# Spectral mixing and a low-rank MLP on one core: x of batches 2 and 3 issued behind a copy of batch 1's a tiles, steps at later slots, x in eight-row pieces

## The chip, the core and the metric

The kernel runs on one core of a Trainium2 chip. A core has a matrix engine (TensorE, PE in the profile, with its weight loads as PEld), a vector engine (VectorE, DVE), an activation engine (ScalarE, ACT), a general engine (GpSimd, POOL) and SyncE (SP), which issues transfers. Each engine works through its own instructions in their order and waits on semaphores for the others. Transfers are issued by SP, ACT or POOL; those issued by POOL form one queue, and POOL alone can change the type of the data on the way. The metric is the device time of one execution in microseconds.

## The reference

For eight batches of x with 3136 rows of 256 values, in float32:

```
X = rfft(x, axis=1);  Y = X * (filt_r + 1j*filt_i);  y = irfft(Y, n=3136, axis=1)
h = (y^T @ U @ V)^T            # U: 3136 x 32, V: 32 x 3136, along the rows
u = y + h
out = u + relu(u @ w_ch1) @ w_ch2      # 256 -> 1024 -> 256
```

## The kernel before

**The transform.** A row number is 49 q + r, with 64 values of q and 49 of r. The transform over q is a product with a constant 64x64 matrix, the one over r a product with one matrix for each of 32 frequencies s. The inverse goes the other way. Everything inside is float16.

**The path of a batch (1 to 7).** It has these stages, and a tile between each two:

- *load_x(b, c)* (lines 147 to 163): a batch's x comes in three chunks c of 8, 8 and 9 positions (`CH`). A tile `xt` has q on 64 partitions for one half h of the positions and 64 for the other. POOL issues one transfer for each half, since the type changes. Position k of half h holds row r = 8*(k//4) + 4*h + k%4 of each q, so that one half's chunk of eight is two pieces of four rows. There are five `xt` buffers.
- *f1_units(b)* (lines 451 to 471): thirteen units, four for each of the first two chunks and five for the last. A unit is one matmul on two positions (`pf`, line 460), and ACT or DVE copies it to `asb`. Behind the last unit of a chunk `asb` is written to the DRAM tensor c1 (line 470), by SP for batch 1 and by POOL for the others.
- *load_a(b, gi)* (lines 477 to 481): SP reads c1 back, the other way round, as four tiles `a` of eight frequencies each. Each has 768 pieces of 512 bytes and a small second transfer; there are three buffers.
- *stream()* (lines 526 to 557): sixteen *pairs* for each batch, one for two frequencies. A pair is the forward product over r (`px`, line 499, one bank of PSUM), the product with the filter on DVE (line 507 for batch 1, lines 518 to 524 for the others, there with a sum on POOL), and, `LAG` = 2 pairs later, the inverse over r (`pi`, line 535), which ACT copies to `esb`. After every fourth pair `esb` is written to the DRAM tensor c2. `stream` is one generator over all batches: each call of `next` makes a pair and the inverse of two pairs before, so the last two inverses of a batch come with the first two pairs of the next.
- *load_e(b, gi)* (lines 483 to 492): SP reads c2 back as the two tiles `e2`.
- *h1_unit(b)* (lines 563 to 600): the product with U, on all of `e2`.
- *make_u* and the MLP: a batch's rows come in six groups of 512 columns. make_u finishes the inverse over q and adds the low-rank part in the same matmul (line 620; lines 629 and 635 for batch 0). mm1 (line 694) makes eight blocks of h, which ACT or DVE passes through relu, and mm2 (line 720, or 765 from batch 2 on) makes the output, which DVE evicts and POOL or SP stores.

**Batch 0** goes another way at the start (`first_f1`, `first_mid`), while the tables, the filters and the weights are loaded. There x of batch 1 is loaded too, V is loaded into two further `xt` buffers (`vq`), and `v_order` (lines 277 to 288) rearranges V with fourteen copies on POOL into `low`. Chunk 0 of batch 2 is issued in the midst of these copies. Copies of w2 follow (line 812).

**The order of the work** is written out by hand. The last loop goes through the groups: for each of four values of a, it emits two blocks of mm1, runs one *slot*, emits mm2 of the group before, and runs a second slot. So a group is eight slots and a batch is `SB` = 48. `put(slot, gen)` hangs one step of a generator on a slot, rounded to the nearest; the steps of one slot run in the order in which they were put. `steps` holds the slots of the pairs; the units, the loads and the h1 steps are put relative to it or at slots of their own:

```
steps = [8.8 + 1.25 * k for k in range(NP)] + [28 + 2.45 * k for k in range(NP)]
...
put(4 + 1.1 * k if b == 2 else 18 + 2.8 * k if b == 3 else t0 - 54 + 3 * k, fill)
...
put(6 * c - 5 if b == 2 else 9 + 8 * c if b == 3 else t0 - 72 + 12 * c, one(load_x, b, c))
```

Slot 0 runs behind the first mm1 of batch 0's first group, at about 55 us of the profile. What a step emits goes to the end of each engine's queue. Seven copies on POOL (line 560) fill the rest of `low`, at slots 8 to 26.

Of the kernel before, what the change touches and what calls it, by code (L numbers as in the profile page):

```python
# [9 lines left out]
F16 = mybir.dt.float16  # L10
# [3 lines left out]
SEQ = 3136  # L14
NQ, NR = 64, 49
NS = 32
# [3 lines left out]
NH = 25  # L20
# [6 lines left out]
def _consts():  # L27
    n, half = SEQ, SEQ // 2
    r = np.array([8 * (k // 4) + 4 * h + k % 4 for h in range(2) for k in range(NH - h)])
    q = np.arange(NQ)  # L30


    w = np.zeros((NQ, NS, 2))
    for s in range(NS):
        w[:, s, 0] = np.cos(2 * np.pi * s * q / NQ)
        w[:, s, 1] = -np.sin(2 * np.pi * s * q / NQ)
    w[:, 0, 1] = (-1.0) ** q
    w = w.reshape(NQ, 64)
    turn = np.arange(64).reshape(4, 16).T.ravel()
    w64 = np.zeros((128, 128))  # L40
    w64[:64, :64] = w
    w64[64:, 64:] = w
    s2 = np.zeros((128, 128))
    s2[:64, :64] = w.T / ESC
    s2[64:, 64:] = w.T / ESC


    t2 = np.zeros((NS, 98, 128))
    g = np.zeros((NS, 128, 98))
    for s in range(NS):  # L50
        for j in range(49):
            if j < 25:
                f = s + 64 * j
                e, sg = np.exp(-2j * np.pi * f * r / n), 1.0
            elif s:
                f = 64 * (j - 24) - s
                e, sg = np.exp(-2j * np.pi * (n - f) * r / n), -1.0
            else:
                f = 32 + 64 * (j - 25)
                e, sg = np.exp(-2j * np.pi * f * r / n), 1.0  # L60
            ei = np.conj(e)
# [12 lines left out]
    t2[0, :, 64] = 0  # L74
    t2[0, 49:, 64] = (-1.0) ** r
# [14 lines left out]
def kernel(  # L90
# [56 lines left out]
    def load_x(b, c, parts=None):  # L147
        if c not in st[b].setdefault("x", {}):
            st[b]["x"][c] = sb.tile([128, 9 * DM], F16, tag="xt", bufs=5, name="xt")
        t = st[b]["x"][c]  # L150
        for lo, hi in parts or ((c0[c], c0[c + 1]),):
            for h in range(2):
                m = (hi - lo) // 4
                nc.gpsimd.dma_start(  # L154
                    t[64 * h:64 * h + 64, (lo - c0[c]) * DM:(lo - c0[c] + 4 * m) * DM]
                    .rearrange("p (m e) -> p m e", m=m),
                    bass.AP(tensor=x.tensor, offset=x.offset + (b * SEQ + 2 * lo + 4 * h) * DM,
                            ap=[[RD, NQ], [8 * DM, m], [1, 4 * DM]]))
# [113 lines left out]
    wp = cst.tile([128, 128], F16)  # L272
    nc.sync.dma_start(wp, wp_d.ap())
    ul = cst.tile([64, NR * RANK], F16)
    hz = [cst.tile([96, DM], F16, tag=f"hz{k}", name="hz") for k in range(2)]

    def v_order():
# [199 lines left out]
    def load_a(b, gi):  # L477
# [2 lines left out]
            nc.sync.dma_start(t[p:p + n].rearrange("p (k d) -> p k d", d=DM), spec(c1[b], gi, p, n))  # L480
        st[b].setdefault("a", {})[gi] = t

    def load_e(b, gi, ks=(0, 1)):
        for k in ks:
            e2 = new_e2(b, k)
            rows_ = c2[b].ap()[16 * gi:16 * gi + 16]
            nc.sync.dma_start(
                e2[gi:64:4, 0:24 * DM].rearrange("p (h e) -> p h e", h=2),
                bass.AP(tensor=c2[b], offset=16 * gi * RD + 12 * k * DM,
                        ap=[[RD, 16], [NH * DM, 2], [1, 12 * DM]]))  # L490
            if k:
                nc.sync.dma_start(e2[gi:64:4, 24 * DM:NH * DM], rows_[:, 24 * DM:NH * DM])
# [33 lines left out]
    def stream():  # L526
        pend = []

        def i1(b, m, y, esb):
            pi = bank("f", "pi")  # L530
            nf = 2 if b == 1 else 1
            for sl in range(2):
                for fi in range(nf):
                    g, o = (fi * NS + 2 * m + sl) * 98, fi * 512 + sl * DM
                    nc.tensor.matmul(pi[0:98, sl * DM:(sl + 1) * DM], g12[:, g:g + 98],  # L535
                                     y[:, o:o + DM], start=(fi == 0), stop=(fi == nf - 1),
                                     skip_group_check=True)
            gi, ml = divmod(m, KG // 2)
            nc.scalar.copy(split(esb[:, ml * 512:(ml + 1) * 512]), natural(pi[0:98, :]))  # L539
            if ml == KG // 2 - 1:  # L540
                for p, n in ((0, 96), (96, 2)):
                    (nc.scalar if b == 1 else nc.sync).dma_start(
                        spec(c2[b], gi, p, n), esb[p:p + n].rearrange("p (k d) -> p k d", d=DM))

        for b in range(1, nb):
            for m in range(NS // 2):
                gi, ml = divmod(m, KG // 2)
                if ml == 0:
                    esb = sb.tile([98, KG * DM], F16, tag="esb", bufs=2, name="esb")
                y = (both_products if b == 1 else product)(m, forward(m, st[b]["a"][gi], ("x",)))  # L550
                if len(pend) == LAG:
                    i1(*pend.pop(0))
                pend.append((b, m, y, esb))
                yield
        for p in pend:
            i1(*p)
            yield

    def one(load, *a):
        load(*a)  # L560
        yield
# [227 lines left out]
    def put(slot, gen):  # L789
        sched.setdefault(int(slot + 0.5), []).append(gen)  # L790
# [13 lines left out]
    nc.vector.tensor_copy(ft[64:65, 0:DM], nyq[64:65, :])  # L804
    for m in range(3):
        first_a(m)
    vgen = v_order()
    for k, _ in enumerate(vgen):
        if k == 3:
            load_x(2, 0)  # L810
    for h in range(2):
        nc.gpsimd.tensor_copy(split(w2)[:, :, h], natural(w2n)[:, :, h])
    fill = f1_units(1, True)
# [8 lines left out]
    for k in range(2):  # L822
        put(k, fill)

    steps = [8.8 + 1.25 * k for k in range(NP)] + [28 + 2.45 * k for k in range(NP)]
    for b in range(3, nb):
        steps += [SB * (b - 2) + 18 + 3 * k for k in range(NP)]
    steps += [steps[-1] + 3 * (k + 1) for k in range(LAG)]
    mid = stream()
    for b in range(1, nb):  # L830
        gen = h1_unit(b)
        for t in (8, 7, 6) if b > 1 else (9, 8, 7):
            put(SB * b - t, gen)
    for k, t in enumerate(steps):
        put(t, mid)
        b, m = divmod(k - LAG, NP)
        if k >= LAG and m % GP == GP - 1:
            t += 6 if b > 1 or not b and m < NP - 1 else 4
            late = SB * b + 13
            if b and t < late:  # L840
                put(max(t, SB * b - 1), one(load_e, b + 1, m // GP, (0,)))
                put(late, one(load_e, b + 1, m // GP, (1,)))
            else:
                put(t, one(load_e, b + 1, m // GP))
    for b in range(1, nb):
        for gi in range(NS // KG):
            t = steps[NP * (b - 1) + GP * gi]
            put(max(2, t - (14 if b > 3 else 9 + b // 3)), one(load_a, b, gi))
        if b > 1:
            fill = f1_units(b, b == 2)  # L850
            t0 = steps[NP * (b - 1)]
            for k in range(NF):
                put(4 + 1.1 * k if b == 2 else 18 + 2.8 * k if b == 3 else t0 - 54 + 3 * k, fill)
            for c in range(len(CH)):
                if b > 2 or c > 0:
                    put(6 * c - 5 if b == 2 else 9 + 8 * c if b == 3 else t0 - 72 + 12 * c, one(load_x, b, c))

    for k in range(7):
        put(8 + 3 * k, one(
# [55 lines left out]
```

## Time and profile before

| | |
|---|---|
| median of 3 runs | 535.67 us (532.67 to 537.13) |
| the profiled execution | 534.16 us, its span 532.4 us |
| busy: PE, DVE, ACT, POOL | 498.4, 400.7, 377.7, 290.9 us |
| the chain that ended last | PE 79%, DVE 6%, POOL 6%, DMA 6% |
| wait of PE's `pf` for xt | 3.0 us in 2 times, the longest 1.9 |
| moved by POOL's queue, by SP's | 41.91 MB, 49.75 MB |
| HBM read and written | 56.25 and 48.17 MB, 196 GB/s over the span |

In a timeline, each row has the start, the time taken, the engine, the line, the operation and tiles, and the number of instructions merged into it; in brackets stands how long the engine had been idle before it, and what ended that. L460 is line 460 of the kernel before. "SPq" is SP as an issuer of transfers. A row of a stretch has its length, and for PE, PEld, DVE, ACT and POOL the busy time with the number of instructions, then the granted clock of PE (1.00 is full), the busy share of the DMA engines and GB/s.

### The profile page before, as it was taken

To read this page: it belongs to the slowest core of one execution; us is meant where nothing else is said; L and a number is where in the kernel's file an instruction comes from. 1 tells how busy PE (TensorE), PEld (TensorE's weight loads), DVE (VectorE), ACT (ScalarE), POOL (GpSimd) and SP (SyncE) were. 2 spreads that over 40 slices of the span, in tenths; PEclk is the share of its full clock that TensorE was granted. 3 is DMA by queue.
4 is the path that set the end of the run, shared out by engine and by line. 5 is a ranking of instruction groups with operands and counts; after the bars stand their busy time and mean duration, and the time that the engine had idled before them with its cause. 6 is when DMAs were issued, how large, how long until landed. Compare 5 with 4: busy or idle time off the path is not lost.

```text
span 532.4 us, 11368 instructions
## 1 busy us (share of the span) xinstructions
PE 498.4 (94%) x4022; PEld 303.0 (57%) x4022; DVE 400.7 (75%) x574; ACT 377.7 (71%) x771; POOL 290.9 (55%) x412
## 2 busy tenths in 40 slices
PE   3877799999999999999999999989999999999995
PEld 3765266667667785555555555545555555454444
DVE  7897367757786758898998888978999877445663
ACT  2767756677678868888788878877777678765541
POOL 7797633345656456586677665765756564313000
PEclk9979989999999999999999999999999999999999
DMA  8989998986988577897989798896887575544324
GB/s 127 193 150 188 204 211 210 217 223 147 232 234 214 141 154 221 208 229 171 225 204 220 195 240 205 177 235 145 199 194 148 126 180 128 140 96 80 78 66 104
DMA packets 118426, 93.98 MB, mean 177 GB/s; under 512 B 52977, under 2 KB 100786, under 8 KB 118370
## 3 DMA queue, kind: packets, MB, share of 16 engines
q0 software_dynamic: 21936, 41.91, 38.3%
q1 hardware_dynamic: 93226, 49.75, 37.7%
q10 hardware_dynamic: 3208, 1.61, 1.1%
q8 instruction: 31, 0.51, 0.4%
q14 instruction: 25, 0.20, 0.1%
HBM read 56.25 MB, written 48.17 MB: 196 GB/s over the span
## 4 chain that ended last, share of the span: by engine, by line
PE 79%; DVE 6%; POOL 6%; DMA 6%; issue 2%; ACT 1%; DVEq 0%; POOLq 0%; ACTq 0%
PE phh L694 27%; PE po L765 21%; PE po L720 8%; PE px L499 5%; PE pi L535 5%; PE pu L620 4%; DVE uv L520 3%; PE pf L460 3%; DMA xt<-in_x_dram 3%; PE ph L577 2%; POOL low L284 2%; DVE uv L518 1%; DMA vq<-in_moe_V_dram 1%; DMA g<-gd 1%; POOL xt L154 1%
## 5 line engine op out<-in xcount | busy, mean ns | idle before, releaser
L702 ACT ACTIVATE h<-phh 128x512 f16<-128x512 f32 (+1 forms) x391 | 205.9, 578 | 71.8 <-PE phh L694 66.9
L694 PE MATMUL phh<-ut,w 128*128 128x512 f16 x768 | 197.6, 379 | 0.6 <-ACT h L702 0.3
L523 POOL TENSOR_TENSOR y<-uv 128x512 f16<-128x512 f16 x96 | 111.0, 1158 | 110.6 <-DVE uv L520 74.8
L765 PE MATMUL po<-h,w 128*128 128x512 f16 x560 | 143.8, 379 | 0.0
L520 DVE TENSOR_TENSOR uv<-px,ft 64x512 f16<-64x512 f32 x192 | 132.1, 688 | 2.6
L694 PEld LDWEIGHTS <-w 128*128 128x128 f16 x832 | 78.5, 98 | 77.2 <-issue 2.4
L518 DVE TENSOR_TENSOR uv<-px,ft 128x512 f16<-128x512 f32 x96 | 65.3, 680 | 42.1 <-PE px L499 35.8
L783 POOL DMA_DIRECT2D out_dram<-och x120 | 70.2, 592 | 42.9 <-DVE och L775 35.6
L539 ACT CAST esb<-pi 98x512 f16<-98x512 f32 x112 | 66.0, 589 | 36.9 <-PE pi L535 33.9
L765 PEld LDWEIGHTS <-w 128*128 128x128 f16 x560 | 51.6, 98 | 53.2 <-issue 1.1
L774 DVE TENSOR_TENSOR tt<-po,ut 128x512 f32<-128x512 f32 x70 | 48.4, 692 | 33.8 <-PE po L765 30.9
L720 PE MATMUL po<-w,h 128*128 128x256 f16 x448 | 58.9, 275 | 0.0
L499 PE MATMUL px<-a,t 98*128 98x256 f16 x256 | 50.0, 277 | 7.2 <-DVE uv L520 3.7
L775 DVE STREAM_TRANSPOSE och<-tt 128x512 f32<-128x512 f32 x70 | 49.8, 711 | 2.4
L466 ACT CAST asb<-pf 128x512 f16<-128x512 f32 (+1 forms) x79 | 45.7, 578 | 5.3 <-PE pf L460 4.2
L720 PEld LDWEIGHTS <-h 128*128 128x128 f16 x448 | 42.8, 98 | 10.8 <-issue 1.4
L507 DVE TENSOR_TENSOR uv<-px,ft 128x1024 f16<-128x1024 f32 x32 | 38.0, 1219 | 13.9 <-PE px L499 13.4
L499 PEld LDWEIGHTS <-t 98*128 98x128 f16 x256 | 23.0, 99 | 33.9 <-DVE uv L520 11.5
L535 PE MATMUL pi<-y,g 128*98 128x256 f16 x192 | 36.7, 271 | 2.0 <-POOL y L523 2.0
L684 ACT CAST ut<-pu 128x512 f16<-128x512 f32 x70 | 38.1, 610 | 0.0
L460 PE MATMUL pf<-xt,w 128*128 128x512 f16 (+1 forms) x91 | 33.4, 373 | 3.3 <-DMA xt<-in_x_dram 3.0
L535 PEld LDWEIGHTS <-g 128*98 128x98 f16 x256 | 29.6, 123 | 4.0 <-issue 2.1
(96 smaller groups left out, 445.0 us busy)
## 6 DMA issues: line engine op xcount, KB each, us to landing
xt<-in_x_dram POOLq DMA_DIRECT2D x46, 256.0 KB, 6.7
a<-c SPq DMA_DIRECT2D x28, 384.0 KB
e<-c SPq DMA_DIRECT2D x56, 192.0 KB
out_dram<-och SPq DMA_DIRECT2D x160, 64.0 KB
c<-esb SPq DMA_DIRECT2D x24, 384.0 KB
c<-asb POOLq DMA_DIRECT2D x30, 256.0 KB, 4.9
out_dram<-och POOLq DMA_DIRECT2D x120, 64.0 KB, 3.2
out_dram<-och POOLq DMA_DIRECT2D x24, 256.0 KB, 4.9
```

The lines of the kernel that those rows point to most:

```text
L499: nc.tensor.matmul(px[:, sl * DM:(sl + 1) * DM], t2[:, s * 128:(s + 1) * 128], a2[:, (2 * ml + sl) * DM:(2 * ml + sl + 1) * DM], start=Tru ...
L518: nc.vector.tensor_mul(uv[:, 0:512], px[:, :], ft[:, a:a + 512])
L520: nc.vector.tensor_mul(uv[p:p + 64, 512:1024], px[q:q + 64, :], ft[q:q + 64, b:b + 512])
L523: nc.gpsimd.tensor_add(y, uv[:, 0:512], uv[:, 512:1024])
L535: nc.tensor.matmul(pi[0:98, sl * DM:(sl + 1) * DM], g12[:, g:g + 98], y[:, o:o + DM], start=(fi == 0), stop=(fi == nf - 1), skip_group_che ...
L539: nc.scalar.copy(split(esb[:, ml * 512:(ml + 1) * 512]), natural(pi[0:98, :]))
L694: nc.tensor.matmul(pm[:, 0:w], w1[:, dh * 1024 + t * 128:dh * 1024 + (t + 1) * 128], ut[:, dh * w:(dh + 1) * w], start=(dh == 0), stop=(dh ...
L702: nc.scalar.activation(h[:, 0:w], pm[:, 0:w], RELU)
L720: nc.tensor.matmul(po[:, o:o + DM], hs[gx, t][:, rr * 128:(rr + 1) * 128], w2[:, t * DM:(t + 1) * DM], start=(t == 0), stop=False, skip_gr ...
L765: nc.tensor.matmul(po[:, :], w2[:, t * DM + dh * 128:t * DM + (dh + 1) * 128], hs[gx, t][:, :], start=(t == 0), stop=(t == 7))
L775: nc.vector.transpose(och.rearrange("p (j h a) -> p h j a", h=2, a=32)[:, dh], tt.rearrange("p (j t) -> p j t", t=32))
L783: (nc.gpsimd if k and b < nb - 1 else nc.sync).dma_start(dst, och[32 * i:32 * i + 32, k * 512:(k + 1) * 512] .rearrange("p (r e) -> p r e" ...
```

## The change

- **x in eight-row pieces.** Position k of half h now holds row 16*(k//8) + 8*h + k%8, so that one half's chunk of eight is one piece of eight rows for each q. The constants of the forward transform follow the new order (`rf`); those of the inverse keep the old one. For batch 0's first chunk, which is loaded in two parts, the parts keep their size.
- **x behind the a tiles.** A new tile `mark` of two values, and `behind(b, gi)`, a copy on POOL from batch b's a tile gi into it. The copy is put ahead of the loads of batch 2's chunk 1 (tile 0), batch 2's chunk 2 (tile 1) and batch 3's chunk 0 (tile 2), in the same slots. POOL reaches these loads only behind the copy, and the copy waits until the tile has landed.
- **Loads of x.** Batch 2's chunk 0 is issued ahead of all copies of `v_order` instead of among them. Batch 2's chunks 1 and 2 are put at slots 3 and 7 (before: 1 and 7), batch 3's at 11, 19 and 27 (before: 9, 17 and 25).
- **Units.** Batch 2's go from 4 + 1.1 k to 5.6 + 1.2 k, batch 3's from 18 + 2.8 k to 20 + 2.8 k.
- **Pairs.** Batch 2's start at slot 30 instead of 28, and from batch 3 on each starts two slots later. Behind batch 1's last pair there are now two steps of their own for its last two inverses, at slots 28.8 and 30.05; the other batches keep them with the next batch's pairs. The loads of a and e follow their pairs; batch 2's a tiles come 8 slots ahead of their pairs (before: 9). The loads of e are put before those of a, x and the units in a slot, as before.

```diff
+    rf = np.array([16 * (k // 8) + 8 * h + k % 8 for h in range(2) for k in range(NH - h)])
...
-                m = (hi - lo) // 4
+                n = min(hi, NH - 1) - lo
                 nc.gpsimd.dma_start(
-                    t[64 * h:64 * h + 64, (lo - c0[c]) * DM:(lo - c0[c] + 4 * m) * DM]
-                    .rearrange("p (m e) -> p m e", m=m),
-                    bass.AP(tensor=x.tensor, offset=x.offset + (b * SEQ + 2 * lo + 4 * h) * DM,
-                            ap=[[RD, NQ], [8 * DM, m], [1, 4 * DM]]))
+                    t[64 * h:64 * h + 64, (lo - c0[c]) * DM:(lo - c0[c] + n) * DM],
+                    rows(x, b, c0[c] + lo + 8 * h, n))
...
+    mark = cst.tile([1, 2], F16)
...
+    def behind(b, gi):
+
+        nc.gpsimd.tensor_copy(mark, st[b]["a"][gi][0:1, 0:2])
...
-        for p in pend:
-            i1(*p)
-            yield
+            while pend and b in (1, nb - 1):
+                i1(*pend.pop(0))
+                yield
...
-    vgen = v_order()
-    for k, _ in enumerate(vgen):
-        if k == 3:
-            load_x(2, 0)
+    load_x(2, 0)
+    for _ in v_order():
+        pass
...
-    steps = [8.8 + 1.25 * k for k in range(NP)] + [28 + 2.45 * k for k in range(NP)]
+    steps = [8.8 + 1.25 * k for k in range(NP + LAG)] + [30 + 2.45 * k for k in range(NP)]
     for b in range(3, nb):
-        steps += [SB * (b - 2) + 18 + 3 * k for k in range(NP)]
+        steps += [SB * (b - 2) + 20 + 3 * k for k in range(NP)]
...
-            put(max(2, t - (14 if b > 3 else 9 + b // 3)), one(load_a, b, gi))
+            put(max(2, t - (14 if b > 3 else (9, 8, 10)[b - 1])), one(load_a, b, gi))
...
-                put(4 + 1.1 * k if b == 2 else 18 + 2.8 * k if b == 3 else t0 - 54 + 3 * k, fill)
+                put(5.6 + 1.2 * k if b == 2 else 20 + 2.8 * k if b == 3 else t0 - 54 + 3 * k, fill)
             for c in range(len(CH)):
+                if (b, c) in ((2, 1), (2, 2), (3, 0)):
+                    put(4 * c - 1 if b == 2 else 11, one(behind, 1, c - 1 if b == 2 else 2))
                 if b > 2 or c > 0:
-                    put(6 * c - 5 if b == 2 else 9 + 8 * c if b == 3 else t0 - 72 + 12 * c, one(load_x, b, c))
+                    put(4 * c - 1 if b == 2 else 11 + 8 * c if b == 3 else t0 - 72 + 12 * c, one(load_x, b, c))
```

More of the change, by code (lines that the diff above doesn't have):

```diff
@@ L51, in _consts @@
         for j in range(49):
+            sg = 1.0
             if j < 25:
                 f = s + 64 * j
-                e, sg = np.exp(-2j * np.pi * f * r / n), 1.0
             elif s:
-                f = 64 * (j - 24) - s
-                e, sg = np.exp(-2j * np.pi * (n - f) * r / n), -1.0
+                f, sg = 64 * (j - 24) - s, -1.0
             else:
                 f = 32 + 64 * (j - 25)
-                e, sg = np.exp(-2j * np.pi * f * r / n), 1.0
-            ei = np.conj(e)
+            fe = f if sg > 0 else n - f
+            e = np.exp(-2j * np.pi * fe * rf / n)
+            ei = np.exp(2j * np.pi * fe * r / n)
             if s:
@@ L74, in _consts @@
     t2[0, :, 64] = 0
-    t2[0, 49:, 64] = (-1.0) ** r
+    t2[0, 49:, 64] = (-1.0) ** rf
     g[0, 64] = 0
@@ L833, with pair @@
             put(SB * b - t, gen)
-    for k, t in enumerate(steps):
+    for t in steps:
         put(t, mid)
[L836 to L844, printed above, removed]
+    def pair(b, m):
+        return NP * (b - 1) + m + (LAG if b > 1 else 0)
     for b in range(1, nb):
         for gi in range(NS // KG):
-            t = steps[NP * (b - 1) + GP * gi]
-            put(max(2, t - (14 if b > 3 else 9 + b // 3)), one(load_a, b, gi))
+            t = steps[pair(b, GP * gi + GP - 1) + LAG]
+            t += 6 if b > 2 or b == 1 and gi < 3 else 4
+            late = SB * (b - 1) + 13
+            if b > 1 and t < late:
+                put(max(t, SB * (b - 1) - 1), one(load_e, b, gi, (0,)))
+                put(late, one(load_e, b, gi, (1,)))
+            else:
+                put(t, one(load_e, b, gi))
+    for b in range(1, nb):
+        for gi in range(NS // KG):
+            t = steps[pair(b, GP * gi)]
+            put(max(2, t - (14 if b > 3 else (9, 8, 10)[b - 1])), one(load_a, b, gi))
         if b > 1:
             fill = f1_units(b, b == 2)
-            t0 = steps[NP * (b - 1)]
+            t0 = steps[pair(b, 0)]
             for k in range(NF):
-                put(4 + 1.1 * k if b == 2 else 18 + 2.8 * k if b == 3 else t0 - 54 + 3 * k, fill)
+                put(5.6 + 1.2 * k if b == 2 else 20 + 2.8 * k if b == 3 else t0 - 54 + 3 * k, fill)
             for c in range(len(CH)):
+                if (b, c) in ((2, 1), (2, 2), (3, 0)):
+                    put(4 * c - 1 if b == 2 else 11, one(behind, 1, c - 1 if b == 2 else 2))
                 if b > 2 or c > 0:
-                    put(6 * c - 5 if b == 2 else 9 + 8 * c if b == 3 else t0 - 72 + 12 * c, one(load_x, b, c))
+                    put(4 * c - 1 if b == 2 else 11 + 8 * c if b == 3 else t0 - 72 + 12 * c, one(load_x, b, c))
     for k in range(7):
```

## The prediction

> **What bounds the kernel now.** I read the shares of the span first, then the span cut into stretches, and then, in the stretch with holes, the timelines of TensorE (PE), GpSimd (POOL) and SyncE (SP).
>
> ```profile
> span 532.4 us, 11368 instructions
> PE 498.4 (94%) x4022; PEld 303.0 (57%) x4022; DVE 400.7 (75%) x574; ACT 377.7 (71%) x771; POOL 290.9 (55%) x412
> ...
> PEclk9979989999999999999999999999999999999999
> ```
>
> PE is busy for 94% of the span, and the change leaves its 4022 matmuls alone. So it can win only PE's 34 us of idle time, and time at the lower granted clock. The stretches say where these lie (first PE busy, then the other engines, then clock):
>
> ```profile
> 40.00:60.00 20.00, 15.62 (x163) 9.04 (x162) 13.09 (x21) 14.25 (x34) 15.84 (x25) 1.00 1.08 204
> 60.00:80.00 20.00, 17.46 (x113) 10.58 (x111) 10.03 (x12) 11.82 (x23) 6.97 (x13) 0.91 0.98 199
> 80.00:100.00 20.00, 19.68 (x152) 14.24 (x150) 14.22 (x16) 13.13 (x25) 7.97 (x15) 1.00 0.81 202
> ```
>
> From 80 us on PE idles little (0.3 us here, 1.1 us in the next 20, 4 us from 200 to 500), so a delay met before 80 us isn't made good behind it. The part edited most is 57 to 72 us, where slots 4 to 10 run:
>
> ```profile
> 57.30 1.08 PE L694 MATMUL phh<-ut,w 128*128 128x512 f16 x4
> 59.53 0.38 PE L460 MATMUL pf<-xt,w 128*128 128x512 f16 x1 [1.15 <-DMA xt<-in_x_dram]
> ...
> 63.28 1.03 PE L694 MATMUL phh<-ut,w 128*128 128x512 f16 x4 [0.31 <-ACT h L702]
> 66.15 0.58 PE L460 MATMUL pf<-xt,w 128*128 128x512 f16 x1 [1.85 <-DMA xt<-in_x_dram]
> 66.53 1.91 PE L720 MATMUL po<-w,h 128*128 128x256 f16 x8
> ...
> 68.45 0.63 PE L499 MATMUL px<-a,t 98*128 98x256 f16 x2
> 68.88 1.25 PE L694 MATMUL phh<-ut,w 128*128 128x512 f16 x4
> 70.40 0.38 PE L499 MATMUL px<-a,t 98*128 98x256 f16 x2 [0.27 <-DVE uv L507]
> ```
>
> The two L460 rows with a DMA behind them are batch 2's forward units 0 (slot 4, chunk 0 of x) and 4 (slot 8, chunk 1): PE waits 1.15 and 1.85 us for x. Behind the second wait the clock is low: eight L720 matmuls take 1.91 us where 70.83 us has 1.03. At 68.45 the first pair of batch 1 starts, with no wait for its a tile. POOL and SP say when x and a were asked for:
>
> ```profile
> 51.79 1.22 POOL L154 DMA_DIRECT2D xt<-in_x_dram  x2
> ...
> 56.16 2.02 POOL L812 COPY w<-w2n 128x1024 f16<-128x1024 f16 x2
> 58.12 1.18 POOL L154 DMA_DIRECT2D xt<-in_x_dram  x2
> 64.24 1.09 POOL L470 DMA_DIRECT2D c<-asb  x2 [4.94 <-ACT ul L296]
> 65.31 1.24 POOL L154 DMA_DIRECT2D xt<-in_x_dram  x2
> ```
> ```profile
> 56.84 1.08 SPq L470 DMA_DIRECT2D c<-asb  x2
> 61.83 4.95 SPq L480 DMA_DIRECT2D a<-c  x6
> ```
>
> x chunk 1 is issued at 58.12, its second half at 58.70; the chain of waits gives that half 7.32 us, so it lands at 66.02. The a tiles can't be asked for before 61.83, since they read what was written from 56.84 on. In the trace's packet records their 512-byte packets start at 63.9, and the 768th, the end of a tile 0, is at about 66.0.
>
> **The change, part by part.**
>
> *Chunk 0 of batch 2 ahead of the low-rank copies.* Its two issues move from 51.8 to about 44.5, ahead of fourteen `low` copies on POOL. They wait there only for PE's fourth unit of batch 1 (44.1). But the queue is first in, first out, behind the w1 and w2n loads, whose packets end at 55.0; x follows at once even now. It lands at 59.4 as before: no gain (bounds 0 and -0.6). The `low` copies end at about 55.0 instead of 56.1, and w2 is ready 0.7 us earlier; nobody waits for either.
>
> *Units of batch 2 from slots 4 + 1.1k to 5.6 + 1.2k.* Unit 0 goes to slot 6, unit 4 to slot 10. The wait of 1.15 us at slot 4 goes. What is late next is ACT, which evicts a bank each 0.58 us there; that leaves 1.0. The wait of 1.85 us at slot 8 goes too, since unit 4 is no longer there. PE then reaches slot 9 (batch 1's first pair) at about 64.6: 57.30 + 1.1 + make_u 1.3 + the two mm1 of slot 6 1.0, then 1.7 us of ACT-paced evictions, unit 2, mm1 1.0 and mm2 1.1.
>
> *Pair 0 now waits.* The a tile lands at about 65.8, as c1's writes and the tile have less x beside them (bounds 65.3 and 66.1, today's). Wait at slot 9: 1.2 us. Its product on DVE (1.23 us) then holds pair 1 for 0.3 more; pair 1 ends at about 67.9.
>
> *Chunk 1 behind the copy of a tile 0.* This adds the wait that decides. On POOL the copy waits for the tile (65.8) and takes under 0.3 us (the smallest POOL row, a memset of 64x256, has 0.31). Behind it in POOL's order stand chunk 1, the copy of tile 1, chunk 2, a `low` copy, the c2 write of chunk 0, the copy of tile 2 and chunk 0 of batch 3. Who waits: unit 4 at slot 10 for chunk 1. From first issue to both halves landed, x took 6.45 us (issued at 32.61, nothing on the hardware queue), 7.6 (51.79), 7.9 (58.12, this chunk), 7.6 (86.16), 8.4 (97.83), 10.2 (127.46). I take 7.4, near this chunk's own row, since tiles 1 and 2 move beside it. Issue at 66.0, landing at 73.4; PE stands at unit 4 from 67.9: 5.5 us. Bounds: one half alone has landed in 4.43 (issued at 324.81); with 0.6 for the second issue that gives a wait of 3.1; 10.2 us give 8.3. Chunk 2, two to three us behind, lands near 76.5 and is needed at slot 15, some 8 us after unit 4: covered. So are a tile 1 (slot 14) and chunk 0 of batch 3 (slot 20).
>
> *Clock.* The windows show 0.91 from 60 to 80 us, which is 3.4 us at half clock; the same work would have been at 67.2 what stands at 70.6 with 1.85 of wait, so this costs 1.6 now. A wait of 5.5 us brings the same again, so the difference is 0, and at most +1.7 if a second such period follows (around 29 to 36 us two follow a wait of 2.4). The Trainium skill (TensorE: Matmul & The Clock Gate, section on HAM oscillation) sets the limit at an idle gap of about 3.4 us. The row disagrees: 1.85 us amid little work sufficed. By the page a wait of under 3.4 us, as in rival 1 below, would bring no half clock, and the sum for that case would be 1.6 lower.
>
> *Later slots.* Batch 1's last two inverses get steps of their own (slots 29 and 30), and batch 2's pairs start at 30. Today pairs stand in slots 27.55 and 28, and PE waits 0.99 us at 104.0 for DVE's uv; that goes: -1.0 (bounds -1.5 and +0.5). From batch 3 on everything is two slots (2.4 us at 57 us per 48 slots) later against the groups. The last e load of a batch is issued at 232.1 and 291.8, and its readers start at 244.7 and 300.8; the packets end about 9 and 6 us ahead, so 2.4 are covered. On SP the first a load of batch 2 moves behind the first e load and some stores move ahead of e loads; the same margin hides these. At 349.9 PE waits 1.95 us for a POOL sum queued behind a store. Two slots may undo this or make another: 0, bounds -2 and +2.
>
> *Eight rows on each half.* As many bytes and issues, half as many pieces. Chunks 1 and 2 of batch 0 land 1.24 us apart for 512 KB read, so they already run at the rate of the engines: 0 (bounds -0.5 and +0.3).
>
> **Sum**: -1.0 - 1.85 + 1.2 + 0.3 + 5.5 - 1.0 = +3.15 us. On the profiled execution's 534.16 us that is 537.3. The median of the runs shown is 535.67, 1.5 above it, so I predict 538.8 as a median.
>
> **Rivals.**
> 1. *x arrives sooner.* With fewer, larger pieces and no other x on the way, chunk 1 lands 4.4 to 5 us after its issue, at 70.7, and the wait is 2.8. For: half a chunk has done it in 4.43. Against: no whole chunk was under 6.45. Net +0.45, so 536.1. The Trainium skill (DMA: Bandwidth & Descriptors, section on the anatomy of one DMA) gives 2.0 us plus bytes at 436 GB/s, an estimate of 4.4 us for 1 MiB read; the trace's 6.45 to 10.2 disagree.
> 2. *Faster.* a and x both come in time, because taking x out of the way brings the a tile early; the waits of slots 4 and 8, their clock loss and the wait at 104.0 all go: -1.0 - 1.85 - 1.6 - 1.0, so 530.2. It decides if chunk 1 lands by 67.9, less than 2 us after the earliest a tile. Nothing in the rows is that fast.
> 3. *Clearly slower.* Chunk 1 takes its longest time (wait 8.3), or the half clock lasts twice: +5.9 or +4.9, with both +7.7, so 540.6 to 543.4. For: two waits close together leave PE idle for most of 8 us.
>
> **Chances.** About what a measurement of this kernel can tell from no change is 1%, 5.4 us. Forecast 0.56, rival 1 0.16, rival 2 0.05, rival 3 0.23. Of the forecast's own case a little lies above 541.0 when the later stages go wrong by 2 us, and of rival 3 some lies below: faster 0.05, same 0.67, slower 0.28. The range takes in rival 1 with a later stage that wins 2 us (534) and rival 3 with all but its end: 533.5 to 543.5.
>
> **What would show it.** Right: no DMA wait at slots 4 and 8, a wait of about 1 us at the first px, and one of 4 to 7 us for xt at an L460 between 67 and 75 us with a low clock behind it; POOL waiting for a until about 66; PE gapless from 80 us on. Wrong: that L460 row without a wait, an a tile landing by 63, or PE waiting for e tiles or POOL sums behind 200 us.

## The result and the profile after

| | before | after |
|---|---|---|
| median | 532.92 us (531.42 to 537.13, 6 runs) | 550.18 us (547.71 to 552.56, 6 runs) |
| ratio, 95% interval | | 1.0306 (1.0259 to 1.0354) |
| profiled execution, its span | 534.16, 532.4 us | 552.56, 550.8 us |

The change makes the kernel 3.1% slower. The forecast was 538.8 us with a range to 543.5. The measured median lies 6.7 us beyond the end of that range, although the sign of the forecast's sum was right. Before's median moved between 532.9 and 535.2 us from one comparison to the next, so from here on ratios are used.

The head of the page of after has the span, the busy shares and the granted clock in 40 slices:

```profile
span 550.8 us, 11362 instructions
...
PE 503.9 (91%) x4022; PEld 305.7 (56%) x4022; DVE 400.0 (73%) x574; ACT 378.0 (69%) x771; POOL 290.4 (53%) x415
...
PEclk9889879999879999999999999999999999999999
```

The span grew by 18.4 us and PE's busy time by only 5.5. So the larger part is new idle time. The clock has a low place in slices 5 and 6 (before: in slice 6; a low place up to slice 3 is in both) and a new one in slices 11 and 12, at 138 to 165 us. The waits of PE by what ended them (total, times, longest) name what stands at both:

```profile
PE px L503 <- DMA a<-c: 8.8, 2, 7.9
...
PE pf L460 <- DMA xt<-in_x_dram: 4.3, 1, 4.3
PE pf L460 <- DVE asb L464: 3.2, 1, 3.2
```

The stretches of after say when (length, PE busy, PEld, DVE, ACT, POOL, then granted clock, DMA share, GB/s):

```profile
40.00:60.00 20.00, 12.66 (x146) 7.79 (x146) 12.31 (x20) 10.82 (x26) 15.24 (x24) 0.96 1.02 187
60.00:80.00 20.00, 14.11 (x73) 7.57 (x72) 5.46 (x7) 10.28 (x21) 6.47 (x15) 0.84 0.81 170
80.00:100.00 20.00, 19.66 (x142) 13.43 (x141) 14.66 (x17) 12.07 (x24) 4.37 (x9) 0.95 0.68 162
100.00:120.00 20.00, 19.87 (x155) 14.24 (x153) 13.24 (x16) 14.12 (x29) 8.43 (x16) 1.00 0.83 228
...
140.00:160.00 20.00, 12.13 (x82) 7.88 (x81) 7.59 (x11) 7.80 (x15) 5.32 (x6) 0.74 0.60 142
```

Two places lose time. Up to 80 us PE is busy 3.0 and 3.4 us less than before in the two stretches shown with the prediction. Then, from 140 to 160 us, it is busy for 12.13 of 20 us at a clock of 0.74, where before it was 18.08 at 1.00:

```profile
140.00:160.00 20.00, 18.08 (x152) 12.86 (x150) 15.76 (x23) 14.11 (x28) 11.29 (x15) 1.00 0.87 236
```

make_u of batch 1 starts at 128.73 us before and at 135.75 after, so 7.0 of the 18.4 us are lost by then and 11.4 behind it. PE's timeline of after shows both places:

```profile
57.90 0.38 PE L460 MATMUL pf<-xt,w 128*128 128x512 f16 x1 [3.23 <-DVE asb L464]
...
70.17 0.39 PE L503 MATMUL px<-a,t 98*128 98x256 f16 x2 [0.98 <-DMA a<-c]
71.87 0.38 PE L503 MATMUL px<-a,t 98*128 98x256 f16 x2 [0.23 <-DVE uv L511]
76.60 0.59 PE L460 MATMUL pf<-xt,w 128*128 128x512 f16 x1 [4.35 <-DMA xt<-in_x_dram]
76.98 1.91 PE L724 MATMUL po<-w,h 128*128 128x256 f16 x8
...
142.37 1.03 PE L698 MATMUL phh<-ut,w 128*128 128x512 f16 x4
151.26 0.58 PE L503 MATMUL px<-a,t 98*128 98x256 f16 x2 [7.87 <-DMA a<-c]
152.07 1.91 PE L724 MATMUL po<-w,h 128*128 128x256 f16 x8
```

The rows from 70.17 to 76.98 are the ones that the prediction described: a short wait at the first pair, a wait of 4.35 us for chunk 1 of x at slot 10, and eight L724 matmuls at half clock behind it. Two were not described. At 57.90 PE waits for a buffer of batch 1's units, and at 151.26 it waits 7.87 us for an a tile of batch 2, with a second half clock (0.61 in 151 to 159 us).

**The wait at 151.26.** It is for batch 2's a tile 2. This is SP's timeline before, with the issue of that tile in its first row:

```profile
116.14 0.96 SPq L480 DMA_DIRECT2D a<-c  x2
124.96 1.87 SPq L542 DMA_DIRECT2D c<-esb  x2
126.93 2.53 SPq L594 DMA_DIRECT2D e<-e  x2
129.51 0.60 SPq L596 DMA_DIRECT2D e<-e  x1
```

And this is SP's timeline after, with it in the last row:

```profile
133.40 1.34 SPq L598 DMA_DIRECT2D e<-e  x2
134.79 0.59 SPq L600 DMA_DIRECT2D e<-e  x1
135.43 0.94 SPq L603 DMA_DIRECT2D e<-e  x1
136.46 2.70 SPq L546 DMA_DIRECT2D c<-esb  x2
139.26 3.26 SPq L480 DMA_DIRECT2D a<-c  x2
```

The load is asked for at 139.26 instead of 116.14. Its slot follows from that of its pair: the pairs moved by two slots and the lead shrank from 9 to 8, so it went from slot 39 to 42. Three slots are 3.6 us at the pace that the prediction used (57 us for 48 slots), but at slot 41 stands the last h1 step of batch 1, whose four e<-e transfers SP issues in its order. SP's waits between 110 and 170 us say what held those, and so what held the load behind them:

```profile
SPq L598 <- DVE e L592: 10.4, 1, 10.4
```

SP stands 10.4 us until DVE has made its copy into `e` (132.69 to 133.37), which has its own place on DVE behind the products of the pairs. Once SP is released, all of it goes out within 10 us. In stretches of after around the wait, the DMA share (the number ahead of the last) goes from 0.43 to full:

```profile
128.00:136.00 8.00, 8.00 (x93) 5.38 (x90) 5.43 (x9) 6.00 (x13) 4.57 (x7) 1.00 0.43 103
136.00:143.00 7.00, 7.00 (x65) 5.00 (x62) 4.88 (x8) 5.38 (x12) 3.37 (x5) 1.00 0.95 208
143.00:151.00 8.00, 0.40 (x2) 0.00 (x0) 0.17 (x1) 1.09 (x2) 1.80 (x3) 0.75 0.96 236
151.00:159.00 8.00, 7.74 (x51) 5.21 (x52) 4.83 (x7) 3.93 (x7) 1.15 (x1) 0.61 0.05 13
```

So the tile takes 12.0 us from its issue to the matmul that reads it, where batch 1's tile 0 takes 4.3 (issue at 65.85, px at 70.17). In before this same tile had the last completion mark of its large transfer 4.3 us after its issue (completion marks are the updates that a transfer makes to its semaphore as its parts land, 16 for this one). The DMA engines stand half idle ahead of the wait, are full while PE stands still, and are nearly empty behind it.

**The wait at 57.90.** DVE's cast into `asb` waits 5.35 us for a write of c1 to finish, and PE then waits 3.23 us for DVE. In this profile SP asks for batch 1's a tiles at 65.85 instead of 61.83. Chunk 0 of batch 2, now issued at 45.36 us, moves beside that write; whether it causes the lateness is asked below.

### The profile page after: what moved, and what is told of

It is laid out like the page before. It is cut to its first block, busy times and chain, and to the rows that moved or that the text cites. A ratio compares the mean times of both kernels' runs of the same rounds, so it can differ in the third digit from the quotient of the medians.

```text
span 550.8 us, 11362 instructions
## 1 busy us (share of the span) xinstructions
PE 503.9 (91%) x4022; PEld 305.7 (56%) x4022; DVE 400.0 (73%) x574; ACT 378.0 (69%) x771; POOL 290.4 (53%) x415
## 4 chain that ended last, share of the span: by engine, by line
PE 73%; DMA 11%; DVE 7%; issue 4%; POOL 4%; SPq 1%; ACT 0%; DVEq 0%; POOLq 0%
PE phh L698 26%; PE po L769 20%; PE po L724 8%; PE px L503 5%; DMA xt<-in_x_dram 5%; PE pi L539 5%; DVE uv L524 4%; PE pu L624 3%; PE pf L460 3%; DMA w2n<-in_moe_w_ch_dram 2%; DMA a<-c 2%; DVE uv L522 2%; PE ph L581 1%; DMA ft<-in_filt_r_dram 1%; PE po L728 1%
## 5 line engine op out<-in xcount | busy, mean ns | idle before, releaser
L527 POOL TENSOR_TENSOR y<-uv 128x512 f16<-128x512 f16 x96 | 113.2, 1180 | 124.4 <-DVE uv L524 87.6
L503 PE MATMUL px<-a,t 98*128 98x256 f16 x256 | 50.8, 281 | 16.4 <-DMA a<-c 8.8
L724 PE MATMUL po<-w,h 128*128 128x256 f16 x448 | 59.8, 278 | 0.0
L724 PEld LDWEIGHTS <-h 128*128 128x128 f16 x448 | 43.3, 99 | 11.7 <-issue 1.4
L503 PEld LDWEIGHTS <-t 98*128 98x128 f16 x256 | 23.2, 100 | 42.5 <-issue 14.0
```

The lines of the kernel that those rows point to most:

```text
L503: nc.tensor.matmul(px[:, sl * DM:(sl + 1) * DM], t2[:, s * 128:(s + 1) * 128], a2[:, (2 * ml + sl) * DM:(2 * ml + sl + 1) * DM], start=Tru ...
L527: nc.gpsimd.tensor_add(y, uv[:, 0:512], uv[:, 512:1024])
L724: nc.tensor.matmul(po[:, o:o + DM], hs[gx, t][:, rr * 128:(rr + 1) * 128], w2[:, t * DM:(t + 1) * DM], start=(t == 0), stop=False, skip_gr ...
```

## The experiments

Two theories stood against each other. **B**: the loss behind 128 us comes from the place of one load on SP's queue. **A**: the loss ahead of it comes from chunk 0 of batch 2, which takes DMA time from c1's first writes; its rival is that the copies on POOL, which hold chunk 1 back, cost the time, as the prediction had it. The first four kernels take these back one by one.

### Chunk 0 of batch 2 back among the low copies

The changed kernel with one edit:

```diff
-    load_x(2, 0)
-    for _ in v_order():
-        pass
+    vgen = v_order()
+    for k, _ in enumerate(vgen):
+        if k == 3:
+            load_x(2, 0)
```

> The changed kernel with one part undone: chunk 0 of batch 2 is issued among the low copies again. Theory 1 (the early issue puts x beside c1's first write of batch 1, which then lands 3 us late, holds the asb buffer, DVE and PE): PE's wait of 3.2 us for DVE's asb near 57 us goes, the first a tile comes 2 to 4 us sooner, and the time falls by 4 to 6 us, to 544 to 546. Rival (the eight-row pieces, which are the larger packets, take the share from c1's write wherever they are issued): the wait stays above 2 us and the time within 2 us of 550.

Measured: 545.99 us, ratio to before 1.0214 (1.0149 to 1.0279). The wait for `asb` is 1.7 us instead of 3.2, the one for the a tile at L503 is still 7.5, the one for chunk 1 is 4.33. The time falls by about 0.9%, as theory A expected, but the intervals of this and the changed kernel overlap, and the wait for `asb` is not gone.

### Batch 2's a tile 2 at its old slot

The changed kernel with this load at slot 39:

```diff
-            put(max(2, t - (14 if b > 3 else (9, 8, 10)[b - 1])), one(load_a, b, gi))
+            early = 3 if (b, gi) == (2, 2) else 0
+            put(max(2, t - early - (14 if b > 3 else (9, 8, 10)[b - 1])), one(load_a, b, gi))
```

> The changed kernel with one load moved: batch 2's a tile 2 is put at slot 39 instead of 42, so that SP issues it ahead of the four transfers of batch 1's h1 step. Theory 1 (PE's wait of 7.9 us near 150 us comes from SP's order, in which that load stands behind transfers that wait for DVE's copy of the h1 step): the wait goes, with the half clock behind it, and the time falls by 8 to 11 us, to 539 to 542. Rival (the tile is late because the DMA engines are busy and pairs are two slots later): a wait of over 4 us for an a tile stays in batch 2, and the time falls by less than 5 us.

Measured: 539.54 us, ratio 1.0102 (1.0032 to 1.0173). The wait at L503 is gone, the one for chunk 1 is still 4.5. The stretch from 140 to 160 us of this kernel:

```profile
140.00:160.00 20.00, 19.55 (x173) 13.83 (x172) 16.07 (x25) 15.12 (x32) 11.20 (x15) 1.00 0.98 229
```

PE is busy 19.55 us at full clock where the changed kernel had 12.13 at 0.74. The slot of one load is worth 2.0 of the 3.1%.

### Both edits

> Both edits at once: chunk 0 of batch 2 among the low copies, and batch 2's a tile 2 at slot 39. Theory 1: the gains add, 535 to 538; what is left above the kernel before is the wait for chunk 1 of x behind the copy of a tile 0, 4 to 5 us at slot 10. Rival (the two losses share a cause, the late start of batch 1): less than the sum of the two, 541 or more.

Measured: 537.51 us, ratio 1.0052 (1.0017 to 1.0086). The load on SP is again worth 1.6% (1.0214 to 1.0052). What is left, 0.5% or 2.8 us, is about the +3.15 us that the prediction had added up; the part on the prediction says how much of that is luck. The profile has the wait for chunk 1 (4.56 us), 1.1 us for the a tile, and still 1.91 for `asb`, with chunk 0 in its old place.

### Both edits, and no copies on POOL

The three calls of `behind` are taken out, so that chunks 1 and 2 are issued as soon as POOL reaches them:

```diff
-                if (b, c) in ((2, 1), (2, 2), (3, 0)):
-                    put(4 * c - 1 if b == 2 else 11, one(behind, 1, c - 1 if b == 2 else 2))
```

> As the kernel with both edits, and the three copies that hold x behind batch 1's a tiles are left out; the loads of x keep their slots, so POOL issues chunks 1 and 2 of batch 2 one after the other near 58 us. Theory 1 (the copy costs: chunk 1 lands 4 us after PE needs it): no wait for x at slot 10, 3 to 5 us less than with the copies, 531 to 534. Rival (the copy protects the a tiles: x beside them delays c1's last write and the first a tile, so that pair 0 waits instead): a wait for an a tile of 3 us or more, and no gain over the kernel with the copies.

Measured: 539.3 us, ratio 1.0098 (1.0056 to 1.014). The wait for x is gone, and the first pair waits instead. A row of this kernel's PE timeline:

```profile
70.19 0.59 PE L503 MATMUL px<-a,t 98*128 98x256 f16 x2 [6.62 <-DMA a<-c]
```

POOL now issues chunks 1 and 2 at 57.6 to 59.7 us, ahead of a tile 0, asked for at 62.96, which takes 7.2 us to the matmul that reads it. The 531 to 534 us that were expected of a mere cost are missed. With the copies it took 4.3 us in the changed kernel, and 3.9 and 4.2 in the one with chunk 0 back and the one with both edits. So the view of the copies as a mere cost fell: given the later units, they exchange a wait for a against one for x, and the exchange is about even, or slightly for the copies.

### Only the copy ahead of chunk 1 taken out, and with four-row pieces

```diff
-                if (b, c) in ((2, 1), (2, 2), (3, 0)):
+                if (b, c) in ((2, 2), (3, 0)):
```

on the kernel with both edits; the second kernel also puts the four-row pieces and their constants back.

> As the kernel with both edits (chunk 0 of batch 2 among the low copies, a tile 2 at slot 39), and of the three copies only the one ahead of batch 2's chunk 1 is left out. Theory 2 (chunk 1 has its place right behind chunk 0, and only chunk 2 and later x must stay behind the a tiles): chunk 1 is issued near 58 us and lands near 66, no wait of 4 us for x at slot 10, and the first a tile comes within 1.5 us of PE; 4 to 6 us less than with all three copies, 530 to 534, as fast as the kernel before or up to 1% faster. Rival (any x beside c1's last write and the a tile costs as much as it saves): a wait of 3 us or more for the a tile, 536 to 540.

> The same kernel with x in four-row pieces, as before the change. Theory 2 (c1's first write of batch 1 lands late because x and w2n stand beside it; the piece's size is of little weight): within 0.5% of the kernel with eight-row pieces. Rival (eight-row pieces take more than their share from c1's write): 2 to 4 us faster than with eight-row pieces, and no wait of PE for DVE's asb near 55 us.

Measured: 535.07 us, ratio 1.0032 (1.0005 to 1.0058), and 534.18 us, 1.0009 (0.9981 to 1.0037). There is no wait for x in either, and the first pair waits 3.75 and 3.90 us for its a tile, with a half clock behind it. The 4.56 and 1.1 us have become one wait of 3.8. This is the best form of the copies that was tried, and it doesn't beat before: theory 2's 530 to 534 us are missed by 1 us, and the wait that its rival expected is there without the rival's time. The piece size made a difference of 0.2%, inside the intervals.

### Chunk 0 early alone, on the kernel before

> The kernel before with one part of the change: chunk 0 of batch 2 is issued ahead of the low copies. Theory 1 (the early chunk delays c1's first write): PE waits 1.5 to 3.5 us for DVE's asb near 55 us, and the kernel is 2 to 5 us slower than before. My prediction on record had no gain and no loss here (0 to -0.6 us): within 0.3% of before.

Measured: 535.95 us, ratio 1.0037 (1.0001 to 1.0072). That is a loss at the edge of what the interval can show. PE waits 1.76 us for `asb` in its profile. Both numbers lie at the lower ends of what theory A expected (2 to 5 us, a wait of 1.5 to 3.5).

### Eight-row pieces alone, twice

> The kernel before with one part of the change: x in eight-row pieces, loads and slots as they were. Theory 2 and the prediction on record: no effect, within 0.4% of before (0, bounds -0.5 and +0.3 us). Rival (larger packets take c1's share): 2 to 4 us slower, with a wait for DVE's asb near 55 us.

> The kernel before with only the eight-row pieces, once more beside the others. If its 0.25% is real: ratio 0.995 to 0.9995. If it was the scatter of the executions: 0.998 to 1.003.

Measured: 532.78 us, ratio 0.9975 (0.9948 to 1.0002), and in a second comparison 533.23 us, 0.9997 (0.9969 to 1.0024). The 0.25% of the first didn't come again. The two profiles are of the same program and settle something else. The first, in DVE's and PE's timelines:

```profile
54.15 1.29 DVE L463 CAST asb<-pf 128x512 f16<-128x512 f32 x2 [2.39 <-DMA c<-asb]
...
68.35 0.38 PE L498 MATMUL px<-a,t 98*128 98x256 f16 x2 [1.03 <-DMA a<-c]
```

The second, with the same two rows:

```profile
56.28 1.29 DVE L463 CAST asb<-pf 128x512 f16<-128x512 f32 x2 [4.51 <-DMA c<-asb]
...
73.60 0.58 PE L498 MATMUL px<-a,t 98*128 98x256 f16 x2 [3.94 <-DMA a<-c]
```

The first of these executions took 532.42 us, the second 538.08. Chunk 0 stands in its old place in both, and yet DVE waits for c1's first write 2.39 us in one and 4.51 in the other, and the a tiles are asked for at 62.28 and 68.35. So that wait scatters between executions of one program. Over all profiles it is 3.88 to 5.35 us in the three kernels with chunk 0 early, and from none to 4.51 us in those with chunk 0 in its old place. So the 5.35 us of the changed kernel's profile can't be put down to the early chunk 0 from this row. What speaks for theory A are the times: the early chunk costs 0.9% (the changed kernel against the first one above), 0.5% (the second against the one with both edits) and 0.4% (alone on before). All three have the same sign, but the intervals of the first two pairs overlap and that of the third begins at 1.0001, so theory A stays open as a small effect.

### The load on SP late, on the kernel before

The counterpart to theory B: only the place of that load is changed, three slots later, and nothing of x, of units or of pairs.

```diff
-            put(max(2, t - (14 if b > 3 else 9 + b // 3)), one(load_a, b, gi))
+            late = 3 if (b, gi) == (2, 2) else 0
+            put(max(2, t + late - (14 if b > 3 else 9 + b // 3)), one(load_a, b, gi))
```

> The kernel before with one load moved: batch 2's a tile 2 is put at slot 42 instead of 39, behind the h1 step of slot 41 as in the changed kernel, so that on SP's queue it stands behind that step's four e copies and a write of c2. Theory (the order on SP alone costs what the changed kernel lost there): issue about 20 us later, near 133 us, a wait of 5 to 9 us at a px of batch 2 between 130 and 150 us with a half clock behind it, +7 to +11 us in the median, ratio 1.013 to 1.021. Rival (the loss needs the early part's delay or the pairs at 30 as well): a wait under 2 us, ratio under 1.005.

Measured: 544.7 us, ratio 1.023 (1.0192 to 1.0269). SP's timeline of this kernel:

```profile
126.62 1.97 SPq L542 DMA_DIRECT2D c<-esb  x2
128.69 2.52 SPq L594 DMA_DIRECT2D e<-e  x2
131.25 0.78 SPq L596 DMA_DIRECT2D e<-e  x1
132.08 0.79 SPq L599 DMA_DIRECT2D e<-e  x1
132.97 1.63 SPq L480 DMA_DIRECT2D a<-c  x2
```

And PE's:

```profile
134.36 1.03 PE L694 MATMUL phh<-ut,w 128*128 128x512 f16 x4
143.85 0.58 PE L499 MATMUL px<-a,t 98*128 98x256 f16 x2 [8.46 <-DMA a<-c]
144.66 1.91 PE L720 MATMUL po<-w,h 128*128 128x256 f16 x8
```

Here SP waits for ACT's copy to `esb` ahead of the write of c2, and the e copies and the load follow. Wait and half clock are close to those of the changed kernel. The load's place costs 2.3% without any other part of the change, a little above the 1.3 to 2.1% expected, and theory B holds. One difference stands beside that: the pair keeps its slot here, so PE comes to it 2.4 us after the load's issue, against 4.1 us in the changed kernel, and a little of the 2.3% is that smaller margin.

### The later part alone, with the old and with the new units

The first kernel keeps the pairs at 30, the two steps of their own, the eight rows and all later slots, with chunk 0 and the units as before, the chunks of batch 2 at slots 1 and 7, no copies, and the load on SP at slot 39. The second differs from it by one line:

```diff
-                put(4 + 1.1 * k if b == 2 else 20 + 2.8 * k if b == 3 else t0 - 54 + 3 * k, fill)
+                put(5.6 + 1.2 * k if b == 2 else 20 + 2.8 * k if b == 3 else t0 - 54 + 3 * k, fill)
```

> The changed kernel with its early part taken back: chunk 0 of batch 2 among the low copies, batch 2's chunks at slots 1 and 7, its units at 4 + 1.1 k, no copies of a tiles, and batch 2's a tile 2 at slot 39. What is left of the change: pairs of batch 2 at 30 and all later ones two slots later, the two steps of their own for batch 1's last inverses, x of batch 3 two slots later, eight-row pieces. Theory (the later slots are worth the 1.0 us wait at 104 us, and the eight rows 0.25%): ratio 0.993 to 0.999. Rival (the later slots win nothing over eight rows alone or lose at a POOL sum): 0.997 to 1.002.

> As w1_late_part, but with batch 2's units at 5.6 + 1.2 k, chunks still at slots 1 and 7. Theory (units later spare PE the waits for x, and no copy holds chunk 1 back; the a tile of the first pair is as late as before): no wait for xt at an L460, a px wait under 2.5 us, ratio 0.992 to 0.999, at or below w1_late_part. Rival (PE reaches the first pair before its a tile lands, since the units no longer fill slots 4 and 5): a px wait of 3 to 4 us with a half clock behind it, ratio 1.000 to 1.004.

Measured: 533.22 us, ratio 0.9995 (0.9961 to 1.0028), and 537.66 us, 1.0073 (1.0044 to 1.0102). The later slots win nothing that can be measured, and the new units, added to them, lose 0.8%; the first fits its rival's range, and the second lies above both ranges given for it. A row of the second kernel's PE timeline has the first pair waiting:

```profile
71.57 0.61 PE L503 MATMUL px<-a,t 98*128 98x256 f16 x2 [4.59 <-DMA a<-c]
```

POOL's order shows a second effect of the units. In the first kernel POOL issues chunk 1 at 60.40, then waits 4.13 us for ACT at the c1 write of batch 2's chunk 0, and issues chunk 2 at 66.61. In the second that write comes with a later unit, behind chunk 2 on POOL, and chunks 1 and 2 go out together from 59.59 on. So the old order held chunk 2 back from the a tiles by a wait on POOL that looks like waste. How much of the 4.59 us this makes is open: in that execution the a tiles were also asked for at 65.81 against 62.32, the scatter of the start-up, and they took 5.8 us, against 5.9 in the first kernel.

## Why the prediction was wrong, step by step

**The step that failed** is the sentence on SP: "On SP the first a load of batch 2 moves behind the first e load and some stores move ahead of e loads; the same margin hides these." It names one load and leaves out another: a tile 2 of batch 2 also moves, behind the e copies of the h1 step and a write of c2. The step weighed it by the margin of other loads. Its own margin was in the trace of before. The tile was asked for at 116.14 and read by the ninth pair of batch 2 (a tile serves four pairs):

```profile
133.56 0.38 PE L499 MATMUL px<-a,t 98*128 98x256 f16 x2
```

The rows that eat this margin were there too. Behind 116.14 SP stands until 124.96 and is through the e copies at about 131. There it asked for the next tile of the batch, tile 3:

```profile
131.69 2.30 SPq L480 DMA_DIRECT2D a<-c  x2
```

The last completion mark of that transfer in the trace is at 141.99, 10.3 us later. A tile 2 in that place would be wanted two slots (2.4 us) behind 133.56, at about 136, and by this estimate would come 5 to 6 us too late. Instead the price was taken as 0; it measured 2.0% (after against the load put back), 1.6% (the same without the early chunk 0) and 2.3% (on the kernel before), 8.5 to 12 us. With it the forecast's +3.15 us would have been some +12 to +15, and the measured difference is 17.3; the rest is of the size of the early chunk 0's 0.4 to 0.9% (2 to 5 us), which is not shown clear of the intervals. "PE gapless from 80 us on" failed for the same reason, at 143 to 151 us.

**Waits at slots 4 and 8**: they go, as said.

**Pair 0**: 1.2 us expected, 0.98 measured, and 0.23 for DVE behind it (0.3 expected). That these agree is partly luck. The last mark of the tile's transfers came at 70.12 instead of 65.8, and PE came to the pair at 69.19 instead of 64.6, both over 4 us late in an execution with the wait for `asb`. The prediction also had today's tile 2 us too early: it took the end of the 768th packet, 66.0, but the packets of tiles 0, 1 and 2 mix there, and tile 0's own marks end at 67.89 and those of its small second transfer at 68.12. In the two kernels without the copy ahead of chunk 1, PE came near the time expected (63.75 and 64.72) and waited 3.75 and 3.90 us.

**Chunk 1 behind the copy**: 5.5 us expected, bounds 3.1 and 8.3; 4.35 measured, and 4.33 to 4.56 in the first three kernels of the experiments, which keep the copy. The mis-sized term is the landing: 6.1 us (issue 70.40, landed 76.47) instead of 7.4. That is below the 6.45 that was the shortest whole chunk before, but far from the 4.4 to 5 of the first rival. POOL's timeline of after shows the step itself, a copy that waited 11.48 us and the load behind it:

```profile
69.91 0.17 POOL L485 COPY mark<-a 1x2 f16<-1x2 f16 x1 [11.48 <-DMA a<-c]
70.40 1.04 POOL L155 DMA_DIRECT2D xt<-in_x_dram  x2 [0.31 <-issue]
```

The prediction counted the copies as a cost with a small gain for pair 0. The runs say more: without them the wait of 4.5 us for x becomes one of 6.6 for a. By these runs, what costs is the combination of later units, which let PE come to the first pair with less work ahead of it, and x and a moving at the same time.

**Clock**: a difference of 0 was taken, at most +1.7. There are low stretches ahead of 60, behind 76 and behind 151 us, where before has one between 60 and 80. The late one came with the failed step (8 us at 0.61). The early ones cost more than the bound: in the kernel with both edits, which has no late one, PE is busy for 501.0 us with the same 4022 matmuls, 2.6 more than before. That a short wait can bring a low clock was read rightly; one length of wait that decides can't be read from the rows. In the kernel with only chunk 0 early, waits of 1.50 and 2.00 us some 3 us apart were followed by 0.61 in the 4 us from 72. In the kernel before with the load late, waits of 1.22 and 1.42 us some 3 us apart were followed by 0.74 in the same 4 us. With eight-row pieces alone (the first profile), waits of 1.32 and 1.03 us, 8 us apart with one of 0.42 between, brought no low clock. The Trainium skill (TensorE: Matmul & The Clock Gate, section on HAM oscillation) puts the limit at an idle gap of about 3.4 us; the measurements stand against it here, where little work lies between the gaps.

**Chunk 0 ahead of the low copies**: no gain, as said. Bounds of 0 and -0.6 left out a loss; +0.4% (0.01 to 0.72) is what the run of it alone shows.

**The wait at 104.0**: it goes, with the 1.0 us expected (PE busy 19.87 of the stretch from 100 to 120 us, 18.89 before). The later part alone gains nothing in its median all the same; an interval of 0.3% (1.8 us) can hide 1 us.

**The e loads and the POOL sum**: inside the bounds. Behind 195 us after has no wait for e tiles. The POOL sum makes PE wait 0.3 us in place of 2.0, but PE's waits for DVE's `uv` there grow from 1.8 to 3.5 us, so the two cancel.

**Eight rows**: 0 expected, ratios of 0.9975 and 0.9997 measured, both with 1 in the interval.

**The rivals.** The third, clearly slower, had the sign and a price of 540.6 to 543.4, by chunk 1's slowest landing or a half clock that lasts twice. The landing was short (6.1 us). The half clock did last nearly twice: the granted clock is 0.52 from 76.0 to 82.4 us, about 6 us at half, against 3.4 before. The first rival needed chunk 1 to land within 5 us and the second by 67.9 us; neither came. No rival had a load on SP.

**The kernel with both edits** is the forecast's own case but for chunk 0, and its +0.5% (2.8 us) is close to +3.15. This too is partly luck: the sum had a longer wait for chunk 1, no cost of the clock and no wait for `asb` (1.91 us in its profile), and the profiled execution, at 540.44, is the slowest of its ten.

What stays open is the price of the early chunk 0, with three values from 0.4 to 0.9% and overlapping intervals, and what a profile of one execution shows of the start-up, which varies as much.

## What to carry to other kernels

When slots move, list every transfer that is put relative to them and, for each, read from the trace of before what it now stands behind on its issuing queue and when that is released: a load that moved three slots (3.6 us) was asked for 17 us later when nothing else was changed (132.97 against 116.14), and 23 us later in the changed kernel, since SP issues in order and passes the longest wait on to everything behind it. Find the instruction that reads that very load by counting, here the pairs, and compare its time with the new issue plus the landing of a load that already stands in that place, not with a neighbour's margin. And before a wait in a queue is taken away as waste, look for what it holds back: here a wait on POOL kept x out of the a tiles' way, and later units were enough to undo it.

## What the runs showed of the hardware

- A load that comes out behind a long-blocked queue was slow as well as late. In the changed kernel and in the kernel before with the load late, the tile took 12.0 and 10.9 us from issue to use, against 3.8 to 7.2 for batch 1's tile 0, with the DMA engines full from issue to use (shares of 0.95 and 1.05 as the views give them). In before, tile 3, which already stood behind the e copies, took 10.3 us to its last completion mark, and tile 2, which stood ahead of them, 4.3. Most a loads of before took 3.4 to 7.5 us, and one, asked for at 192.24, 12.2. That the transfers released together are the cause is argued from these rows; no run isolates it.
- The last of a transfer's completion marks can come late. In the trace's records of the changed kernel, 15 of the 16 marks of that tile's large transfer are there at 147.97 us, and the last at 150.65. PE's matmul also waits for the tile's small second transfer, whose last mark is at 151.13, and starts at 151.26. So over 3 us of the wait pass with one mark of each transfer outstanding. In the kernel before with the load late, the 16th mark came 1.5 us behind the 15th.
- The same program's a tiles of batch 1 were asked for at 62.28 us in one execution and 68.35 in another, and the executions took 532.42 and 538.08 us. One profile of the start-up is one draw: the wait for `asb` that stood out in the changed kernel's profile can't be told from this scatter.
